# Block attention with a gated convolution MLP in fp32r on one Trainium2 core: units of 512 tokens without halo instead of 288 tokens with it

## The chip, the cores and the metric

One core of one Trainium2 chip runs the kernel. The metric is the device time of one execution in microseconds (us), from several executions of the compiled program; beside it one execution was recorded by the hardware profiler. Engines: TensorE (PE), VectorE (DVE), ScalarE (ACT), GpSimd (POOL), and SyncE (SP), whose queue issues all DMAs here. PSUM has eight banks of 512 fp32 columns; SBUF holds everything else.

## The reference

q, k and v are (8, 8, 576, 64): batch, heads, tokens, head width. Each chunk of 64 tokens attends to itself, and the heads side by side are the input (512 wide) of an MLP with a gate from a convolution over three tokens, which stops at the ends of each batch entry (576 tokens):

```python
scores = scale * np.matmul(q_c, k_c.transpose(0, 1, 2, 4, 3))     # 64 x 64 per chunk and head
attn = softmax(scores)                                            # max taken away, sum + 1e-9
x = (attn @ v_c), heads side by side                              # (8, 576, 512)
h = np.maximum(x @ w_in, 0.0)                                     # (8, 576, 1024)
conv_out[s] = sum over k of conv_w[k] * hp[s + k]                 # hp: h with a zero token at both ends
out = h * (1 / (1 + np.exp(-conv_out))) @ w_out                   # (8, 576, 512)
```

w_in, conv_w and w_out come as 64-bit floats and are split on the chip; the outputs are fp32.

## The kernel before, in words

The kernel works on 36 tiles of 128 tokens for the attention and the output, and on 16 units of 288 tokens (half a batch entry, `UNITS`, L49) for the first product and the gate. All 4608 tokens lie in one row.

Both products run in fp32r with each operand split into a high and a low half, three matmuls for one: high x high, high x low, low x high. The first product (`mm1`, L352) of a unit u and a block f of 128 of the 1024 hidden columns is 3 x 4 matmuls with wi as weights and x as moving tile; its 290 columns are the 288 tokens and 2 of the neighbour unit (`x_window`, L322), since the convolution needs the token beside. The result lies in one PSUM bank. From there: `h_relu` (ACT, in place), `c_mid` (ACT, middle tap), `c_left` and `c_right` (DVE, outer taps), `c_sig` (ACT, tanh of half), `c_mul` (DVE, (tanh + 1) * h, which frees the bank), `g_hi` (ACT, rounds to fp32r), `g_lo` (POOL, the rest, which frees the buffer c). g_h and g_l are rings of 640 tokens for each block (`GR`, L47). The second product (`mm2`, L410) of a tile t and a block f is three matmuls with 128 tokens of g as weights and 512 columns of wo as moving tile; eight steps f sum a tile up in one bank. `o_copy` (ACT) and `o_store` (SP) bring it out.

Attention of a tile: its q and k are turned (the first nine tiles on TensorE, `t_pe`, L170; later ones on DVE, `t_dve`), `scores` (L219: 32 matmuls of 64x64), softmax (`s_max`, `s_sub`, `s_sum`, `s_eps`, `s_rec` on DVE, `s_exp` on ACT, `s_norm`, `s_fold`, `s_scale` on POOL), the weights turned (on TensorE, `p_pe`; from tile 12 by DMA and DVE, `p_swap`, `p_dve`), `attn_v` (L302: 32 matmuls of 64x64), and `x_hi` (ACT) and `x_lo` (DVE) write the unit's moving tiles x_h and x_l, three units in turn (`NX`). A PSUM tile of two banks, `sx`, has two halves, each for the scores or the product of one tile. From tile 12 on a second one is lent from the banks (`give_up`, L212), and one step `both` (L316) multiplies the last pair with v and makes the scores of the next.

The weights (4 MB each of w_in and w_out as 64-bit words) are loaded and converted in the first 60 us: `w_load` (SP), `w_scale`, `w_hi` (ACT), `w_shift`, `w_words` (DVE), `w_left_g` (POOL).

What sets the order: `step` (L76) collects all steps with engine, buffers taken and freed, and the steps that they come after; `order_` (L751) is a list of their numbers written out by hand, which fixes the order of the instructions on each engine, SP's queue among them. The loop behind it (L875) hands out the buffers in that order (`room`, L516) and computes from planned costs where spare matmuls on the identity fill early idle time (L926, L929). Each engine takes its instructions strictly in this order.

Of the kernel before, what the change touches and what calls it, by code (L numbers as in the profile page):

```python
# [18 lines left out]
def attn_ffn(ctx: ExitStack, tc: tile.TileContext, q, k, v, w_in, conv_w, w_out, out):  # L31
# [10 lines left out]
    HS = S // 2  # L42
    CUTS0 = [0, HS]
    XU = HS + 2
    XS = XU + 2
    NX = 3
    GR = 5 * P  # L47
    NT = B * S // P
    UNITS = [(c0, c1) for b in range(B) for c0, c1 in zip(CUTS0 if b == 0 else [S * b, S * b + HS], (CUTS0 if b == 0 else [S * b, S * b + HS])[1:] + [S * b + S])]  # L49
    NU = len(UNITS)  # L50
    W_ROWS = set()
    NAT = 9
    TG = 3
    BOTH = 12
    PAIR = 12
    ONE_PAIR = True
# [6 lines left out]
    rawv = ctx.enter_context(tc.tile_pool(name="rawv", bufs=4))  # L63
    work = ctx.enter_context(tc.tile_pool(name="work", bufs=2))
    work3 = ctx.enter_context(tc.tile_pool(name="work3", bufs=3))
    work4 = ctx.enter_context(tc.tile_pool(name="work4", bufs=4))
    work1 = ctx.enter_context(tc.tile_pool(name="work1", bufs=1))
    work7 = ctx.enter_context(tc.tile_pool(name="work7", bufs=7))
# [18 lines left out]
    ps_y = ExitStack()  # L87
# [10 lines left out]
    x_h = const.tile([P, NX, KT, XS], F32R, name="x_h")  # L98
    x_l = const.tile([P, NX, KT, XS], F32R, name="x_l")
    g_h = const.tile([P, FT, GR], F32R, name="g_h")  # L100
    g_l = const.tile([P, FT, GR], F32R, name="g_l")
    cw = const.tile([P, 3 * FT], F32, name="cw")

# [97 lines left out]
    def sx_half(i):  # L201

        cols = slice(G * C * (i % 2), G * C * (i % 2) + G * C)
        return (sx if i // 2 else lent["pair"])[:, :, cols]
# [3 lines left out]

    def lend(st):
        pass  # L210

    def give_up(st):  # L212

        st["given"] = st.get("given", 0) + 1
        if st["given"] == 2:
            ps_y.close()
            st["pair"] = ctx.enter_context(tc.tile_pool(name="ps_z", bufs=1, space=PSUM)).tile([P, 2, 512], F32, name="z_ps")

    def scores(st):  # L219
# [18 lines left out]
    def s_sub(st):  # L238
        st["e"] = work3.tile([P, H, C], F32, name="e")
# [62 lines left out]
    def attn_v(st):  # L302
        for g in range(G):
            for s in range(2):
                for hp in range(2):
                    j0, n, m = C * (hp ^ s), hp, s
                    if st["t"] >= TP:
                        j0, n, m = C * s, hp, hp if st["t"] >= TP + 2 else hp ^ s
# [7 lines left out]
    def both(st, tiles, tiles_x):  # L316
        for a in tiles_x:
            attn_v(a)
# [3 lines left out]
    def x_window(u):  # L322

        a, z = UNITS[u]
        return a - (2 if a % S else 0), z + (2 if z % S else 0)

    def x_views(st, t, x):

        xv = sx_half(st.get("x", 2)).rearrange("p s (g i) -> p g s i", i=C)
        parts = []  # L330
        for s in range(2):
            t0 = C * (2 * t + s)
            for u in range(NU):
# [89 lines left out]

# [546 lines left out]
```

## Time and profile before

| | us |
|---|---|
| median of 3 executions | 492.94 |
| lowest and highest | 489.9, 494.02 |
| span of the profiled execution, first to last instruction | 488.9 |
| TensorE busy in it | 478.4 (98%) |
| VectorE, ScalarE, GpSimd busy | 342.6 (70%), 299.2 (61%), 192.0 (39%) |

The profiled execution has no time of its own beside its span; the median of the executions is 4.0 us longer than the span. Matmuls are pipelined and their ends are modelled, so lengths of neighbouring matmuls overlap; what one costs is the distance of the starts. An engine's busy time says little about an engine that is not the bound.

### The profile page before, as it was taken

The page shows a single profiled execution, that of the slowest core. Times are in us where ns is not written, and L with a number is a line of the kernel's source. Part 1 is how long each engine was busy: PE and PEld are TensorE (multiplying, and loading weights), DVE is VectorE, ACT ScalarE, POOL GpSimd, SP SyncE. Part 2 cuts the span into 40 slices and gives each one's busy share as a digit, 9 for nine tenths or more (in the row PEclk, how much of TensorE's full clock was granted, in tenths as well). Part 3 has the DMA queues.
Part 4 walks back from the last instruction along what each step waited for, and adds up shares of the span by engine and source line. Part 5 has one row for each costly group of instructions (what it writes and reads, how often), then busy time and mean ns, then how long its engine had stood idle before and what let it go on. Part 6 is the DMA issues. An engine that isn't in the chain of part 4 may idle for free.

```text
span 488.9 us, 12846 instructions
## 1 busy us (share of the span) xinstructions
PE 478.4 (98%) x4961; PEld 425.2 (87%) x4961; DVE 342.6 (70%) x726; ACT 299.2 (61%) x749; POOL 192.0 (39%) x261
## 2 busy tenths in 40 slices
PE   7799999999999999999999999999999999999996
PEld 4689899989899889898898999998889899998885
DVE  3789988767877788888778687978786655563300
ACT  4589997667564656765556566655654566565411
POOL 1245565252351635355242525352523155143120
PEclk9899999999999999999999999999999999999999
DMA  8998955234655744266565444547302002010012
GB/s 214 297 271 214 269 96 81 48 49 89 131 114 112 147 84 98 47 143 131 101 132 101 100 79 76 118 95 165 82 23 83 24 6 66 0 44 1 21 66 86
DMA packets 180610, 50.16 MB, mean 103 GB/s; under 512 B 164653, under 2 KB 172869, under 8 KB 180549
## 3 DMA queue, kind: packets, MB, share of 16 engines
q1 hardware_dynamic: 180548, 49.34, 44.2%
q8 instruction: 39, 0.64, 0.6%
q14 instruction: 23, 0.18, 0.1%
HBM read 36.72 MB, written 9.44 MB: 94 GB/s over the span
## 4 chain that ended last, share of the span: by engine, by line
PE 90%; DMA 4%; ACT 2%; DVE 2%; POOL 1%; issue 1%; SPq 0%; POOLq 0%; ACTq 0%
PE b_ps L414 42%; PE b_ps L360 39%; DMA qk<-in_k 3%; PE sx_ps L309 2%; PE sx_ps L226 2%; PE b_ps L177 2%; PE z_ps L309 1%; DMA w<-in_moe_w_out 1%; PE z_ps L226 1%; PE b_ps L295 1%; DVE wt L456 1%; POOL wi_l L460 1%; ACT wt L447 0%; ACT c L372 0%; SPq L121 0%
## 5 line engine op out<-in xcount | busy, mean ns | idle before, releaser
L405 POOL TENSOR_TENSOR g_l<-c,g_h 128x288 fp32r<-128x288 f32 (+8 forms) x184 | 110.1, 620 | 184.9 <-ACT g_h L401 155.6
L414 PE MATMUL b_ps<-wo_h,g_h 128*128 128x512 f32 x288 | 115.6, 402 | 0.0
L414 PE MATMUL b_ps<-wo_h,g_l 128*128 128x512 f32 x288 | 113.6, 394 | 0.0
L414 PE MATMUL b_ps<-wo_l,g_h 128*128 128x512 f32 x288 | 113.4, 394 | 0.0
L376 DVE SCALAR_TENSOR_TENSOR c<-b_ps,cw,c 128x287 f32<-128x287 f32 (+1 forms) x128 | 64.7, 509 | 55.1 <-ACT c L372 54.7
L360 PE MATMUL b_ps<-x_h,wi_h 128*128 128x290 f32 x512 | 90.3, 298 | 0.2 <-ACT qkT L195 0.2
L360 PE MATMUL b_ps<-x_l,wi_h 128*128 128x290 f32 x512 | 89.6, 297 | 0.0
L367 ACT ACTIVATE b_ps<-b_ps 128x290 f32<-128x290 f32 x128 | 50.8, 399 | 63.1 <-PE b_ps L360 62.8
L360 PE MATMUL b_ps<-x_h,wi_l 128*128 128x290 f32 x512 | 89.2, 296 | 0.0
L360 PEld LDWEIGHTS b_ps<-x_h,wi_h 128*128 128x128 f32 x512 | 80.2, 189 | 9.2 <-ACT qkT L195 0.4
L391 DVE SCALAR_TENSOR_TENSOR c<-c,b_ps 128x288 f32<-128x288 f32 x128 | 56.7, 446 | 35.7 <-ACT c L388 35.2
L388 ACT ACTIVATE c<-c 128x288 f32<-128x288 f32 x128 | 56.6, 444 | 41.0 <-DVE c L382 40.1
L360 PEld LDWEIGHTS b_ps<-x_l,wi_h 128*128 128x128 f32 x512 | 75.8, 190 | 0.0
L360 PEld LDWEIGHTS b_ps<-x_h,wi_l 128*128 128x128 f32 x512 | 75.4, 189 | 0.0
L372 ACT ACTIVATE c<-b_ps,cw 128x288 f32<-128x288 f32 x128 | 63.9, 501 | 9.7 <-POOL g_l L405 2.4
L382 DVE SCALAR_TENSOR_TENSOR c<-b_ps,cw,c 128x288 f32<-128x288 f32 (+1 forms) x128 | 64.8, 512 | 2.8
L414 PEld LDWEIGHTS b_ps<-wo_h,g_l 128*128 128x128 f32 x288 | 54.2, 188 | 12.7
L401 ACT CAST g_h<-c 128x288 fp32r<-128x288 f32 (+8 forms) x184 | 58.3, 355 | 7.1 <-PE b_ps L414 3.6
L414 PEld LDWEIGHTS b_ps<-wo_h,g_h 128*128 128x128 f32 x288 | 54.4, 189 | 8.6
L414 PEld LDWEIGHTS b_ps<-wo_l,g_h 128*128 128x128 f32 x288 | 54.2, 188 | 7.5
L271 POOL TENSOR_TENSOR wt<-wt,z 128x512 f32<-128x512 f32 x24 | 25.3, 1053 | 45.9 <-DVE z L262 18.6
L419 ACT ACTIVATE wt<-b_ps 128x512 f32<-128x512 f32 x36 | 21.4, 597 | 31.2 <-PE b_ps L414 31.1
(66 smaller groups left out, 467.8 us busy)
## 6 DMA issues: line engine op xcount, KB each, us to landing
out<-wt SPq DMA_DIRECT2D x36, 256.0 KB, 2.4
v<-in_v SPq DMA_DIRECT2D x21, 256.0 KB, 3.5
qk<-in_q SPq DMA_DIRECT2D x96, 48.0 KB, 2.3
qk<-in_k SPq DMA_DIRECT2D x96, 48.0 KB, 2.2
w<-in_moe_w_out SPq DMA_DIRECT2D x4, 1024.0 KB, 6.4
wt<-wt SPq DMA_DIRECT2D x48, 64.0 KB, 2.0
qk<-in_k SPq DMA_DIRECT2D x96, 24.0 KB, 1.9
qk<-in_q SPq DMA_DIRECT2D x96, 24.0 KB, 1.9
```

The lines of the kernel that those rows point to most:

```text
L271: nc.gpsimd.tensor_tensor(out=two(st, "to"), in0=two(st, "of"), in1=z, op=ALU.mult)
L360: nc.tensor.matmul(h_ps[:, 0:hi - lo], lhsT=wt[:, f // 2, kt, P * (f % 2):P * (f % 2) + P], rhs=xt[:, u % NX, kt, 0:hi - lo], start=n == 0 ...
L367: nc.scalar.activation(out=h, in_=h, func=AF.Relu)
L372: nc.scalar.mul(out=st["c"], in_=banks[st["h"]][:, i0:i0 + st["n"]], mul=cw[:, FT + f:FT + f + 1])
L376: nc.vector.scalar_tensor_tensor(out=c[:, a:n], in0=banks[st["h"]][:, i0 + a - 1:i0 + n - 1], scalar=cw[:, f:f + 1], in1=c[:, a:n], op0=AL ...
L382: nc.vector.scalar_tensor_tensor(out=c[:, 0:b], in0=banks[st["h"]][:, i0 + 1:i0 + 1 + b], scalar=cw[:, 2 * FT + f:2 * FT + f + 1], in1=c[: ...
L388: nc.scalar.activation(out=st["c"], in_=st["c"], func=AF.Tanh, scale=0.5)
L391: nc.vector.scalar_tensor_tensor(out=st["c"], in0=st["c"], scalar=1.0, in1=banks[st["h"]][:, st["i0"]:st["i0"] + st["n"]], op0=ALU.add, op ...
L401: nc.scalar.copy(out=g_h[:, f, gs], in_=st["c"][:, cs])
L405: nc.gpsimd.tensor_tensor(out=g_l[:, f, gs], in0=st["c"][:, cs], in1=g_h[:, f, gs].bitcast(F32), op=ALU.subtract)
L414: nc.tensor.matmul(banks[st["o"]], lhsT=gt[:, f, o:o + P], rhs=wt[:, f, :], start=f == 0 and n == 0, stop=f == FT - 1 and n == 2)
L419: nc.scalar.mul(out=st["os"], in_=banks[st["o"]], mul=0.5)
```

## The change

The first product's units become 9 units of 512 tokens, four attention tiles each, with no neighbour tokens. Its matmuls have 512 columns and fill a bank; in unit 0 a block is made in two halves of 256 columns, the first of which needs tiles 0 and 1 only. The passes over a block run on the whole bank. The outputs of the tokens at a unit's ends, and of those beside a batch boundary within a unit, are made by another way: `rim_ends` and `rim_mid` (ACT) copy two tokens at each such place of h into a small tile `rim`, and once per unit `rim_steps` does the convolution, the gate and the split for four tokens in eight blocks at once with small operations (POOL: `r_mid`, `r_side`, `r_add`, `r_lo`; ACT: `r_sig`, `r_hi`; DVE: `r_mul`). The output tiles begin one token before a unit's tiles; the first and the last tokens share one tile, which is stored in two transfers at the end.

x_h and x_l keep two units instead of three, each row of 512 columns, so that all large tiles begin at one place mod 256 bytes (a row of x_h was 292 columns, 1168 bytes). The second `sx` tile is gone: scores and product of a pair are steps of their own, and all six other banks serve the products throughout. Pairs begin at tile 4. Buffers: c 7 to 3, wt 4 to 3, v 4 to 3, e 3 to 2, and two for the output (`os`). `order_` is a new list: the rows of tile 0 are loaded ahead of w_in, and the second product of a unit, up to four tiles in turn, stands between the first-product blocks of the next.

```diff
-    HS = S // 2
-    NX = 3
-    GR = 5 * P
+    UT = 4
+    UN = UT * P
+    NU = NT // UT
...
-    x_h = const.tile([P, NX, KT, XS], F32R, name="x_h")
-    g_h = const.tile([P, FT, GR], F32R, name="g_h")
+    x_h = const.tile([P, 2, KT, UN], F32R, name="x_h")
+    g_h = const.tile([P, FT, UN + P], F32R, name="g_h")
+    rim = const.tile([P, FT, 8 * NU + 8], F32, name="rim")
...
-    def both(st, tiles, tiles_x):
-        for a in tiles_x:
-            attn_v(a)
+    def scores_of(tiles):
         for a in tiles:
             scores(a)
+    def attn_of(tiles):
+        for a in tiles:
+            attn_v(a)
...
-    def mm1(st, u, f):
+    def mm1(st, u, f, c0, c1):
         n = 0
         for wt, xt in ((wi_h, x_h), (wi_h, x_l), (wi_l, x_h)):
             for kt in range(KT):
                 nc.tensor.matmul(
-                    h_ps[:, 0:hi - lo], lhsT=wt[:, f // 2, kt, P * (f % 2):P * (f % 2) + P], rhs=xt[:, u % NX, kt, 0:hi - lo],
+                    banks[st["h"]][:, c0:c1], lhsT=wt[:, f // 2, kt, P * (f % 2):P * (f % 2) + P], rhs=xt[:, u % 2, kt, c0:c1],
                     start=n == 0, stop=n == 3 * KT - 1)
...
+    def rim_ends(st, u, f):
+        h, r = banks[st["h"]].rearrange("p (a b) -> p a b", b=2), rim[:, f, 8 * u:8 * u + 8].rearrange("p (a b) -> p a b", b=2)
...
+            nc.scalar.copy(out=r[:, 0:4:3, :], in_=h[:, 0:UN // 2:UN // 2 - 1, :])
+    def rim_mid(st, u, f):
+        m = (S - UN) * u
+        n = min(m + 2, UN) - (m - 2)
+        nc.scalar.copy(out=rim[:, f, 8 * u + 2:8 * u + 2 + n], in_=banks[st["h"]][:, m - 2:m - 2 + n])
...
+    def r_add(st, k, n):
+        i = slice(0, 2) if n == 0 else slice(k // 2, k // 2 + 1)
+        c = st["rc"][:, :, n, i]
+        nc.gpsimd.tensor_tensor(out=c, in0=c, in1=st["rt"][:, :, n, i], op=ALU.add)
...
     def o_store(st, t):
-        nc.sync.dma_start(out=out_rows[P * t:P * t + P, :], in_=st["os"])
+        if t is None:
+            nc.sync.dma_start(out=out_rows[0:P - 1, :], in_=st["os"][1:P, :])
+            nc.sync.dma_start(out=out_rows[P * NT - 1:P * NT, :], in_=st["os"][0:1, :])
+            return
+        nc.sync.dma_start(out=out_rows[t:t + P, :], in_=st["os"])
...
-    room = {"slot": 2, "wslot": 2, "sx": 4, "bk": 6, "grp": 2, "v": 4, "qkT": 2, "m": 2, "e": 3, "z": 2, "pT": 2, "c": 7, "wt": 4,
-            "wv": 2, "we": 1}
+    room = {"slot": 2, "wslot": 2, "sx": 2, "bk": 6, "grp": 2, "v": 3, "qkT": 2, "m": 2, "e": 2, "z": 2, "pT": 2, "c": 3, "wt": 3, "os": 2, "rc": 2}
...
+    def attend(tiles, writes):
+        sts = [st_ for st_, _, _, _ in tiles]
...
+        s = step("PE", 0.47 * len(tiles), key, scores_of, (sts,), [a for _, tt, _, _ in tiles for a in tt],
+                 take=[("sx", st_, "s") for st_ in sts], free=["qkT"] * len(tiles), bank="sx")
+        ends = soft_all(sts, s, key)
+        s = step("PE", 0.47 * len(tiles), key, attn_of, (sts,), [a for a in ends] + [v_ for _, _, v_, _ in tiles],
+                 take=[("sx", st_, "x") for st_ in sts], free=["pT", "v"] * len(tiles), bank="sx")
+        for st_ in sts:
+            t = st_["t"]
+            a = step("ACT", 0.58, key + 1, x_hi, (st_, t), [s] + writes, bank="sx")
+            x_done[t] = step("DVE", 0.69, key + 1, x_lo, (st_, t), [a], free=[("sx", "x")], bank="sx")
...
     def block(key, u, f, after):
+        if u == 0:
+            s = step("PE", 1.43, key, mm1, (st, u, f, 0, UN // 2), wi_done[f] + [x_done[0], x_done[1]], take=[("bk", st, "h")])
+            s = step("PE", 1.43, key, mm1, (st, u, f, UN // 2, UN), [s, x_done[2], x_done[3]])
+        else:
+            s = step("PE", 2.73, key, mm1, (st, u, f, 0, UN), wi_done[f] + [x_done[t] for t in range(UT * u, UT * u + UT)], take=[("bk", st, "h")])
...
+        s = g = step("ACT", 0.62 if u else 0.8, key + 2.5, g_hi, (st, u, f), [s] + [mm2_of[u - 1, j, f] for j in range(UT) if (u - 1, j, f) in mm2_of])
+        s = step("POOL", 1.37 if u else 1.55, key + 2.5, g_lo, (st, u, f), [s], free=["c"], port=True)
...
+    sets = [[t] for t in range(4)] + [[t, t + 1] for t in range(4, NT, 2)]
...
     order_ = [
-        0, 30, 12, 72, 91, 31, 32, 33, 13, 1, 14, 77, 15, 73, 16, 36, 74, 75, 2, 4, 17, 3, 92, 76, 110, 5, 6,
+        71, 0, 1, 72, 2, 90, 3, 4, 5, 6, 74, 7, 11, 73, 75, 12, 17, 8, 9, 91,
...
```

In the new list, decoded: TensorE's order in the head is the turning of tiles 0 to 5, the scores of tiles 0 to 3, the products of tiles 0 to 2, the first half block (f = 1), the product of tile 3, the next half block. SP's order is the rows of tile 0, conv_w, the rows of tile 1, the two halves of the first quarter of w_in, the rows of tile 2, v of 0, the rows of 3, half of the second quarter, v of 1, the other half, the rows of 4 and 5, v of 2, the third quarter, v of 3, the last quarter, the rows of 6, v of 4, half of w_out, v of 5, the rows of 7, the other half of w_out, v of 6, the rows of 8. Between a pair's product with v and the next pair's scores stand, from tile 12 on, four steps of the second product, or one block of the first product, or more of both. The last unit's first-product blocks end 18 steps of the second product before the first step that needs `rim_steps` of that unit.

## Rows read from the trace of the kernel before

**Rows 1.** The page of the profile, its head: the span, and each engine's busy time with its share of the span and its count of instructions.

```profile
span 488.9 us, 12846 instructions
...
PE 478.4 (98%) x4961; PEld 425.2 (87%) x4961; DVE 342.6 (70%) x726; ACT 299.2 (61%) x749; POOL 192.0 (39%) x261
```

**Rows 2.** The table by stage: the stretch in us and its length, busy time of PE, PEld (weight loads), DVE, ACT and POOL with their counts, the granted TensorE clock, the busy share of the DMA engines and the GB/s that they moved.

```profile
0.00:20.00 20.00, 14.30 (x173) 9.84 (x175) 10.62 (x22) 9.61 (x15) 4.04 (x10) 0.98 0.92 261
20.00:40.00 20.00, 19.23 (x334) 17.07 (x331) 15.73 (x31) 16.45 (x31) 9.77 (x7) 0.94 0.95 268
40.00:60.00 20.00, 19.75 (x308) 17.93 (x307) 19.10 (x41) 19.26 (x43) 11.15 (x9) 1.00 0.98 237
60.00:80.00 20.00, 20.00 (x187) 18.40 (x187) 17.01 (x36) 18.10 (x45) 11.82 (x11) 1.00 0.54 95
...
200.00:240.00 40.00, 40.00 (x466) 35.84 (x465) 32.72 (x69) 24.26 (x62) 19.00 (x29) 1.00 0.55 114
```

**Rows 3.** The chain that ended last, in order of time: start in us, length in us, what it is and of how many instructions.

```profile
135.74 4.84 PE b_ps L360 x36
...
225.35 5.58 PE b_ps L414 x24
...
461.30 23.81 PE b_ps L414 x102
```

**Rows 4.** The timeline of TensorE in the head: start in us, length in us, line, what it writes and reads, shape, count, and in brackets idle time before it with its releaser. L177 and L182 turn q and k, L360 is the first product.

```profile
8.67 2.98 PE L177 MATMUL b_ps<-ident,qk 128*64 128x128 f32 x48 [1.62 <-DMA qk<-in_k]
...
17.88 4.40 PE L177 MATMUL b_ps<-ident,qk 128*64 128x128 f32 x48 [2.37 <-DMA qk<-in_k]
...
31.60 0.78 PE L360 MATMUL b_ps<-x_h,wi_h 128*128 128x290 f32 x4
...
37.74 0.60 PE L182 MATMUL b_ps<-ident,qk 128*128 128x128 f32 x4
38.09 0.78 PE L360 MATMUL b_ps<-x_h,wi_h 128*128 128x290 f32 x4
```

**Rows 5.** The costliest groups of the page, the first third of each product: line, engine, operation, out<-in, shape, count, then busy us, mean ns of one, and idle time before. The two other thirds of each product have the same counts.

```profile
L414 PE MATMUL b_ps<-wo_h,g_h 128*128 128x512 f32 x288 | 115.6, 402 | 0.0
...
L360 PE MATMUL b_ps<-x_h,wi_h 128*128 128x290 f32 x512 | 90.3, 298 | 0.2 <-ACT qkT L195 0.2
```

**Rows 6.** The timeline of TensorE around one visit to the attention (L309 the product with v, L226 the scores, two tiles of each).

```profile
218.12 0.40 PE L414 MATMUL b_ps<-wo_h,g_l 128*128 128x512 f32 x1
218.45 0.69 PE L309 MATMUL z_ps<-pT,v 64*64 64x64 f32 x32
...
219.43 0.65 PE L226 MATMUL sx_ps<-qkT 64*64 64x64 f32 x32
219.90 0.65 PE L226 MATMUL z_ps<-qkT 64*64 64x64 f32 x32
220.47 0.50 PE L414 MATMUL b_ps<-wo_h,g_h 128*128 128x512 f32 x1
220.81 0.39 PE L414 MATMUL b_ps<-wo_l,g_h 128*128 128x512 f32 x1
```

**Rows 7.** The timeline of SP's queue in the head: each row is the issue of DMAs.

```profile
0.73 0.96 SPq L434 DMA_DIRECT2D w<-in_moe_w_in  x2
1.73 0.76 SPq L121 DMA_DIRECT2D qk<-in_q  x1
...
10.76 0.63 SPq L121 DMA_DIRECT2D qk<-in_q  x1
```

**Rows 8.** Groups of instructions of the other engines, shapes kept apart: columns as in rows 5. L372, L376 and L391 are passes over a block, L401 and L405 make g_h and g_l, L345 and L349 make x_h and x_l, L460 makes the low half of a weight.

```profile
L372 ACT ACTIVATE c<-b_ps,cw 128x288 f32<-128x288 f32 x128 | 63.9, 501 | 9.7 <-POOL g_l L405 2.4 <-ACT b_ps L367 0.4
...
L391 DVE SCALAR_TENSOR_TENSOR c<-c,b_ps 128x288 f32<-128x288 f32 x128 | 56.7, 446 | 35.7 <-ACT c L388 35.2
...
L376 DVE SCALAR_TENSOR_TENSOR c<-b_ps,cw,c 128x288 f32<-128x288 f32 x64 | 32.4, 508 | 31.7 <-ACT c L372 31.5
...
L349 DVE TENSOR_TENSOR x_l<-sx_ps,x_h 128x512 fp32r<-128x512 f32 x14 | 9.3, 673 | 3.8 <-ACT x_h L345 3.8
...
L345 ACT CAST x_h<-sx_ps 128x512 fp32r<-128x512 f32 x14 | 8.2, 592 | 2.9 <-PE sx_ps L226 2.6 <-PE sx_ps L309 0.2
...
L349 DVE TENSOR_TENSOR x_l<-sx_ps,x_h 128x256 fp32r<-128x256 f32 x13 | 5.2, 415 | 0.7 <-ACT x_h L345 0.7
L460 POOL TENSOR_TENSOR wi_l<-wt,wi_h 128x512 fp32r<-128x512 f32 x4 | 5.1, 1291 | 11.1 <-DVE wv L479 8.5 <-ACT qkT L193 1.9 <-DVE wt L456 0.7
...
L405 POOL TENSOR_TENSOR g_l<-c,g_h 128x32 fp32r<-128x32 f32 x16 | 4.1, 254 | 12.4 <-ACT g_h L401 12.4
...
L401 ACT CAST g_h<-c 128x32 fp32r<-128x32 f32 x16 | 3.4, 213 | 1.0 <-DVE c L391 0.7
```

**Rows 9.** The costliest groups of the page: all pieces of g_l and of g_h, of several lengths.

```profile
L405 POOL TENSOR_TENSOR g_l<-c,g_h 128x288 fp32r<-128x288 f32 (+8 forms) x184 | 110.1, 620 | 184.9 <-ACT g_h L401 155.6
...
L401 ACT CAST g_h<-c 128x288 fp32r<-128x288 f32 (+8 forms) x184 | 58.3, 355 | 7.1 <-PE b_ps L414 3.6
```

**Rows 10.** The timeline at the end, ScalarE: the last two output tiles are copied.

```profile
484.44 1.30 ACT L419 ACTIVATE wt<-b_ps 128x512 f32<-128x512 f32 x2 [0.75 <-PE b_ps L414]
```

**Rows 11.** The timeline of ScalarE behind the visit of rows 6: the casts to x_h of the two tiles that were multiplied there.

```profile
223.40 0.59 ACT L345 CAST x_h<-z_ps 128x512 fp32r<-128x512 f32 x1
...
226.08 0.59 ACT L345 CAST x_h<-sx_ps 128x512 fp32r<-128x512 f32 x1
```

More of the change, by code (lines that the diff above doesn't have):

```diff
@@ L578, in att @@
-        if old:
-            s = step("PE", 0.47 * len(new + old), key, both, (new[0][0], [n[0] for n in new], [o[0] for o in old]), after,
-                     take=take, free=free, bank="sx")
-        else:
-            s = step("PE", 0.47, key, scores, (st,), after, take=take, free=free, bank="sx")
-        before["s"] = s
-        for b, tb, _, writes_b in old:
-            x_steps(b, tb, s, key, writes_b)
-        if t == PAIR - 1:
-            a = step("POOL", 0.0, key, give_up, (lent,), [s], take=[("bk", lent, ("y", 0))])
-            step("POOL", 0.0, key, give_up, (lent,), [a], take=[("bk", lent, ("y", 1))], free=[("sx", "l0"), ("sx", "l1")])
@@ L589, in att @@
[L589 to L603 removed]
+        return st, tt, ldv
@@ L637, in x_steps @@
[L637 to L643 removed]
+            return [step("POOL", 1.05, key + 3, s_scale, (st,), [n], free=["z"], port=True)]
@@ new lines, in attn_ffn @@
+        for set_ in sets:
+            if u < NU and set_[0] // UT == u:
+                writes = [mm1_of[u - 2, f] for f in range(FT)] if u > 1 else []
+                tiles = [(*att(t, key_of[t], 0.1 + 0.5 * t if t < 5 else 4.5 + t), key_of[t]) for t in set_]
+                attend(tiles, writes)
+        for f in range(FT):
+            if u < NU:
+                g_of[u, f] = block(U[u] + (U[u + 1] - U[u]) * f / FT, u, f, [])
+        if u and u < NU:
+            rim_steps(U[u + 1] + 3, u)
@@ L735, in attn_ffn @@
+    st, prev = {}, None
+    for f in range(FT):
+        key = U[NU] + 40 + 0.7 * f
+        prev = step("PE", 0.68, key, mm2, (st, UN, f), [prev, g_of[0, f][1], rim_done[NU - 1, 1]] + wo_done[f], take=[("bk", st, "o")] if f == 0 else [])
+    s = step("ACT", 0.6, key + 1, o_copy, (st,), [prev], take=["os"], free=[("bk", "o")])
+    step("SP", 0.9, key + 2, o_store, (st, None), [s], free=["os"], lag=0.8)
     early = {"DVE": 0.083, "ACT": 0.092, "PE": 0.0, "POOL": -0.075, "SP": -0.05}
     late = {"DVE": 0.035, "ACT": 0.035, "PE": 0.035, "POOL": 0.1, "SP": 0.1}
-    kinds = {scores: 1, attn_v: 1, both: 1, p_pe: 2, t_pe: 2, c_pe: 2}
+    kinds = {scores_of: 1, attn_of: 1, p_pe: 2, t_pe: 2, c_pe: 2}
```

332 lines of the change are left out of this document (147 added, 185 removed), and 219 rows, old and new, of the table order_.

## The prediction

> **What bounds the kernel now.** I read the busy shares and slices first, then the table by stage, then the chain that ended last, then single stretches. The page says that TensorE is busy 98% of a span of 488.9 us, with the next engine, VectorE, at 70% [rows 1]. A busy matmul row is modelled and overlaps its neighbour, so busy alone proves little. What proves it is the stages: from 60 us to 470 us TensorE has no idle time in any window (20.00 of 20.00, 40.00 of 40.00), while in 200 to 240 us VectorE works 32.72 of 40, ScalarE 24.26 and GpSimd 19.00 [rows 2]. And in the chain in order of time the long pieces are runs of the two products: 36 matmuls of 290 columns in 4.84 us, 24 of 512 in 5.58 us, 102 of 512 in 23.81 us [rows 3]. So the kernel is a row of matmuls without gaps from 31.6 us, where the first product begins [rows 4], to 485 us, with a head before and a tail of some 4 us behind. The head is the only stretch with another limit: the DMA engines are busy 92% to 98% for the first 60 us at 237 to 268 GB/s [rows 2], and TensorE waits there for q and k (2.37 us before 17.88 us) [rows 4].
>
> From these pieces one matmul of the first product costs 4.84/36 = 134.3 ns and one of the second 5.58/24 = 232.5 ns from start to start. There are 3 x 512 and 3 x 288 of them [rows 5]: 206.3 us and 200.9 us.
>
> The time is the median 492.9 us, the span of the profiled execution 488.9 us; I take the 4.0 us between them as unchanged and work in differences.
>
> **First product, 290 to 512 columns.** Of 1536 matmuls, 960 remain: 8 units x 8 blocks x 12 = 768 of 512 columns, and 192 of 256 in unit 0, whose blocks are cut in two. No row shows this product at 512 columns. Granted clock 1.00 [rows 2] is the 2.4 GHz level, 0.417 ns a cycle; if a column takes one cycle, 290 columns take 120.8 ns and 13.5 ns come on top. Lower end: this surplus is per matmul, so 512 columns cost 213.3 + 13.5 = 226.8 ns. Upper end: it is per column, 134.3 x 512/290 = 237.1 ns. The second product's row, 232.5 ns, lies between, with a surplus of 19.2 ns. I take 226.8 ns: same weights, same moving tile, and 13.5 ns is already a mean over starts at every multiple of 16 bytes, since a row of x_h is 1168 bytes now. At 256 columns, 106.7 + 13.5 = 120.2 ns. 768 x 0.2268 + 192 x 0.1202 = 174.2 + 23.1 = 197.3 us, so -9.0 us (ends: 237.1 and 118.5 ns, -1.5; 224, -11).
>
> **Second product, tiles at one place mod 256 bytes.** Count and width stay. By the shapes, x_h and x_l are 14016 bytes, 192 over a multiple of 256, so g_h now stands 128 bytes off wo_h; afterwards all big tiles begin at one place. No row shows that this place costs anything: the surplus of 19.2 against 13.5 ns may be place or width. Ends: 226.8 ns (-4.9 us) if place is all of it, 232.5 (0) if none, 238 (+4.9) if the common place is the worse one. I take half, -2.5 us.
>
> The Trainium skill (TensorE: Matmul & The Clock Gate, section Back-to-back issue gap) gives N/2.4 + 2.5 ns for a warm matmul, 123 ns at 290 columns and 216 ns at 512. The trace disagrees: 134.3 and 232.5 ns. By that page's figures the two products would together take some 373 us after the change, an estimate; what would have to hold for it is the last rival below.
>
> **Attention steps.** Scores and the product with v now go in separate steps of one pair. Each visit to the 64x64 matmuls costs beyond its work: the matmul before it is followed after 0.33 instead of 0.23 us, the first one after it is followed after 0.34 instead of 0.23, and the last group is stretched (219.90 to 220.47 us, 0.57 where the group before it takes 0.47) [rows 6]: about 0.33 us. Before there are 12 + 11 + 13 = 36 visits, afterwards 20 + 20 = 40: +1.3 us.
>
> **Head.** The rows of tile 0 are now loaded ahead of w_in; before, 1 MB of w_in is issued first, at 0.73 us [rows 7], about 4 us of DMA at 261 GB/s [rows 2]. Tile 0 is turned from 8.67 us, and tile 2, whose load waits for its place until 10.76 us, only at 17.88 us [rows 4, 7]; both should come some 3 to 4 us earlier. The first half-width block needs only tiles 0 and 1 instead of 0 to 2. Against this, the new order of TensorE has the attention of tile 3 right after the first half block, and its v is the 7.0th MB in the queue: at 257 GB/s it lands near 29.5 us. By then TensorE has also done what now comes behind 31.6 us: tile 5 turned (two times four transposes, 0.35 us for four from start to start), four more transposes, and a half block of 1.4 us [rows 4]. So it stands 2.1 us earlier with 2.5 us more done, 4.6 us ahead, of which waits for the v of tile 5 (11.0 MB) and the rows of tiles 7 and 8 take back about 1.8. ScalarE and VectorE work 80% to 96% of 20 to 60 us [rows 2] and convert the weights in the same time, so I book -2 us (ends -5 and +2).
>
> **Work of the other engines** does not grow. At 512 columns an x_h cast takes 0.59 us, x_l 0.67 us, and 256 columns fewer save 0.26 us [rows 8]. From this slope three VectorE passes make 0.74 + 0.74 + 0.67 = 2.15 us for a block, x72 = 155 us, where 128 x (0.51 + 0.51 + 0.45) = 188 us is spent now; ScalarE four passes of about 0.63 plus two rim copies of 0.21, 2.9 us x72 = 211 us, where 128 blocks x four passes of 0.36 to 0.50 us stand now, 184 to 256 us; GpSimd 1.29 us (the row of w_left at 512) x72 = 93 against 110 us, plus 8 rounds of about nine small operations near 0.25 us, 18 us in all [rows 8, 9]. None is on the path: TensorE spends some 48 us on a unit (96 matmuls of each product, 44 us, and four tiles of attention). The rim round itself stands, on GpSimd, in front of the last two g_lo of its unit and in the last unit in front of two output tiles; there 18 steps of the second product (12 us) lie between the last first-product block and the first step that needs it, and its chain is about 10 us. Cost 0; without this cover 2 us once.
>
> **Waits that the change adds.** The pair's scores share two halves of one PSUM tile with the product before them, so scores wait until x_lo of the pair before is done. Queued behind on TensorE is everything. The order leaves 12 matmuls of 512 columns, 2.7 us, at seven places and 3.4 us or more at the rest; two x_h and two x_l take 2.5 us [rows 8]. I book 2 us for 16 pairs. Buffers c go from 7 to 3; a c is held about 5.4 us by the durations above, so three serve a block each 1.8 us, below the 2.7 us of a block. Behind a c_mid that waits for one stand ScalarE's casts and o_copy; the price is 0 while TensorE has second-product steps in between, and is bounded by the slower rival.
>
> **Tail.** Now ScalarE copies the last two tiles (484.44 us, 1.30 us) and SP stores [rows 10]; afterwards the last two tiles end together and the last store is two transfers: +0.5 us.
>
> Sum: -9.0 - 2.5 + 1.3 - 2 + 2 + 0.5 = -9.7 us, span 479.2, time 483.2 us.
>
> **Rivals.**
> *Nothing from width or place.* Both products at 232.5 ns, head unchanged: -4.6 + 0 + 1.3 + 0 + 2 + 0.5 = -0.8, time 492. For it: 232.5 is the only row of this width, in the tail too, where nothing else runs (23.81/102 = 233.4 ns). Against: the first product's surplus is smaller.
> *Larger gain.* A common place takes the second product to 226.8 as well, the head gives 5, scores never wait: -9.0 - 4.9 + 1.3 - 5 + 0.5 = -17.1, time 476. For it: the head is bound by what is loaded first.
> *Slower: scores wait for x_lo.* Place: between a pair's product with v and the next scores. In before the pair multiplied at 218.45 us is cast only at 223.40 and 226.08 us, because casts stand in ScalarE's order behind other work [rows 6, 11]; there nothing waits for it. If the second x_lo comes 4.5 us after the product, TensorE loses 1.75 us at seven places and about 1.1 at nine, 22 us in place of my 2: +10.3, time 503. It decides from 0.73 us a pair (11.7/16). Against: in 200 to 240 us VectorE has 18% and ScalarE 39% free [rows 2].
> *The surplus was all place.* With one place for all tiles a matmul would cost only its columns: 184.3 us for each product, -22.0 - 16.6 + 1.8 = -36.8, time 456. Against: a surplus stands in both rows, with fixed and with changing places. The formula of the Trainium skill's page on TensorE (section Back-to-back issue gap) would come nearest to this.
>
> **Chances.** Forecast (478 to 488) 0.55, of which 0.02 within 1%; nothing from width 0.13; larger gain 0.20; scores wait 0.09; all place 0.03. A measurement of this kernel tells about 1% from no change, 4.9 us. Faster 0.53 + 0.20 + 0.03 = 0.76, same 0.15, slower 0.09. The range 474 to 492 leaves out the last two rivals.
>
> **What would show it.** Runs of first-product matmuls in the chain at 2.72 us for 12 (2.79 if width gives nothing); runs of 24 second-product matmuls at 5.44 to 5.51 us instead of 5.58; the first product starting at 26 to 30 us; idle time of TensorE before the scores lines, released by x_lo, below 2 us in all. Idle TensorE of over 10 us behind 60 us, or matmuls of 512 columns at 237 ns, would prove the forecast wrong.

## The result and the profile after

The changed kernel is slower by 0.7%: 495.9 us against 492.7 us in the median of 13 runs each, ratio 1.0072 (95% interval 1.0055 to 1.009). One of the runs before took 937.9 us; it does not enter the ratio. The forecast was 483, the range 474 to 492, so the time lies outside and on the other side. In the profiled executions the span went from 488.9 [rows 1] to 494.9 us, 6.0 us where the medians differ by 3.2. In every run with both numbers the time is 1.8 us longer than the span (496.71 and 494.9 us for the one profiled here), so the 488.9 us belong to about 490.7 us, a run 2.0 us below its median: of the 4.0 us between median and span before, only 1.8 are fixed. Differences of single spans below are uncertain by some 2 us for this reason.

The page's head and the table by stage (columns as in rows 2):

```profile
span 494.9 us, 11257 instructions
...
PE 470.2 (95%) x4383; PEld 387.5 (78%) x4383; DVE 318.2 (64%) x554; ACT 273.6 (55%) x617; POOL 176.5 (36%) x229
```

```profile
0.00:20.00 20.00, 15.06 (x199) 11.67 (x203) 9.14 (x21) 8.57 (x15) 3.67 (x10) 0.99 0.75 219
20.00:40.00 20.00, 17.32 (x361) 15.03 (x357) 12.98 (x23) 13.71 (x23) 6.96 (x6) 0.93 0.94 240
...
200.00:240.00 40.00, 40.00 (x294) 32.77 (x293) 30.76 (x56) 24.49 (x59) 18.56 (x25) 1.00 0.41 85
...
481.00:483.00 2.00, 0.00 (x0) 0.00 (x0) 0.00 (x0) 0.00 (x0) 0.00 (x0) 1.00 0.40 138
483.00:490.00 7.00, 0.00 (x0) 0.00 (x0) 0.00 (x0) 0.00 (x0) 0.00 (x0) 0.55 0.06 23
490.00:493.00 3.00, 0.00 (x0) 0.00 (x0) 0.00 (x0) 0.00 (x0) 0.00 (x0) 0.50 0.07 26
```

TensorE is busy 8 us less than before, as it was meant to be, and still the span is longer. The last three rows say where: behind 481 us no engine computes, and from 483 to 493 us the DMA engines are busy 6 to 7% at 23 to 26 GB/s. One sixteenth is 6.25%, the share of one DMA engine of 16 at work. The timelines (SyncE in the head, TensorE at the first product and around one visit to the scores, ScalarE, TensorE and SyncE at the end) and the chain in order of time:

```profile
8.94 0.61 SPq L98 DMA_DIRECT2D qk<-in_q  x1
...
32.80 0.74 PE L308 MATMUL b_ps<-x_h,wi_h 128*128 128x256 f32 x4
...
222.89 0.39 PE L427 MATMUL b_ps<-wo_h,g_l 128*128 128x512 f32 x1
223.20 1.16 PE L191 MATMUL sx_ps<-qkT 64*64 64x64 f32 x64
224.30 0.50 PE L427 MATMUL b_ps<-wo_h,g_h 128*128 128x512 f32 x1
224.63 0.39 PE L427 MATMUL b_ps<-wo_l,g_h 128*128 128x512 f32 x1
...
479.67 1.28 ACT L432 ACTIVATE os<-b_ps 128x512 f32<-128x512 f32 x2 [4.84 <-PE b_ps L427]
479.87 0.39 PE L427 MATMUL b_ps<-wo_h,g_l 128*128 128x512 f32 x1
...
480.97 0.26 SPq L436 DMA_DIRECT2D out<-os  x1
481.29 4.13 SPq L437 DMA_DIRECT2D out<-os  x1
```

```profile
353.96 8.16 PE b_ps L308 x36
...
426.54 8.16 PE b_ps L427 x36
```

TensorE's last matmul in the kernel before:

```profile
484.70 0.40 PE L414 MATMUL b_ps<-wo_h,g_l 128*128 128x512 f32 x1
```

Both products now run at 8.16/36 = 226.7 ns a matmul, where the second took 232.5 before [rows 3]. TensorE's last matmul ends at 480.3 us, 4.8 earlier than before (485.1). From there to the end of the span it is 14.6 us instead of 3.8. The store issued at 480.97 us is the last output tile that is stored: 127 rows from partition 1 on; the one issued at 481.29 is its partition 0, the last token.

### The profile page after: what moved, and what is told of

It is laid out like the page before. It is cut to its first block, busy times and chain, and to the rows that moved or that the text cites. A ratio compares the mean times of both kernels' runs of the same rounds, so it can differ in the third digit from the quotient of the medians.

```text
span 494.9 us, 11257 instructions
## 1 busy us (share of the span) xinstructions
PE 470.2 (95%) x4383; PEld 387.5 (78%) x4383; DVE 318.2 (64%) x554; ACT 273.6 (55%) x617; POOL 176.5 (36%) x229
## 4 chain that ended last, share of the span: by engine, by line
PE 81%; DVE 7%; DMA 4%; ACT 3%; issue 2%; SPq 0%; POOL 0%; ACTq 0%
PE b_ps L427 38%; PE b_ps L308 34%; PE sx_ps L274 3%; PE sx_ps L191 3%; DMA qk<-in_k 2%; PE b_ps L154 1%; DMA v<-in_v 1%; DVE c L345 1%; DMA w<-in_moe_w_in 1%; DVE c L361 1%; DVE c L351 1%; DVE m L201 1%; ACT g_h L372 1%; DVE wt L469 1%; DVE wt L464 0%
## 5 line engine op out<-in xcount | busy, mean ns | idle before, releaser
L376 POOL TENSOR_TENSOR g_l<-c,g_h 128x510 fp32r<-128x510 f32 (+1 forms) x80 | 79.2, 998 | 178.3 <-ACT g_h L372 115.7
L308 PE MATMUL b_ps<-x_h,wi_h 128*128 128x512 f32 (+1 forms) x320 | 80.7, 374 | 0.9 <-ACT qkT L172 0.6
L308 PE MATMUL b_ps<-x_l,wi_h 128*128 128x512 f32 (+1 forms) x320 | 78.8, 368 | 0.0
L308 PE MATMUL b_ps<-x_h,wi_l 128*128 128x512 f32 (+1 forms) x320 | 78.7, 368 | 0.0
L345 DVE SCALAR_TENSOR_TENSOR c<-b_ps,cw,c 128x510 f32<-128x510 f32 x72 | 53.1, 740 | 36.2 <-ACT c L340 28.7
L361 DVE SCALAR_TENSOR_TENSOR c<-c,b_ps 128x510 f32<-128x510 f32 (+1 forms) x72 | 48.1, 672 | 29.2 <-ACT c L357 21.7
L308 PEld LDWEIGHTS b_ps<-x_h,wi_h 128*128 128x128 f32 x320 | 56.1, 188 | 11.8 <-ACT qkT L172 0.9
L427 PEld LDWEIGHTS b_ps<-wo_h,g_h 128*128 128x128 f32 x288 | 54.1, 188 | 11.9
L427 PEld LDWEIGHTS b_ps<-wo_h,g_l 128*128 128x128 f32 x288 | 54.1, 188 | 11.5
L357 ACT ACTIVATE c<-c 128x510 f32<-128x510 f32 (+1 forms) x72 | 45.5, 635 | 20.7 <-DVE c L351 20.4
L351 DVE SCALAR_TENSOR_TENSOR c<-b_ps,cw,c 128x510 f32<-128x510 f32 (+1 forms) x72 | 53.0, 740 | 2.1 <-ACT rim L325 0.7
L372 ACT CAST g_h<-c 128x510 fp32r<-128x510 f32 (+1 forms) x80 | 44.9, 578 | 16.9 <-DVE c L361 13.0
L340 ACT ACTIVATE c<-b_ps,cw 128x510 f32<-128x510 f32 (+1 forms) x72 | 49.6, 692 | 1.8 <-ACT b_ps L315 0.4
L432 ACT ACTIVATE os<-b_ps 128x512 f32<-128x512 f32 x36 | 21.4, 601 | 31.3 <-PE b_ps L427 27.7
```

Of the source, the lines that this page charges most:

```text
L308: nc.tensor.matmul(banks[st["h"]][:, c0:c1], lhsT=wt[:, f // 2, kt, P * (f % 2):P * (f % 2) + P], rhs=xt[:, u % 2, kt, c0:c1], start=n == ...
L340: nc.scalar.mul(out=st["c"], in_=banks[st["h"]][:, i0:i0 + n], mul=cw[:, FT + f:FT + f + 1])
L345: nc.vector.scalar_tensor_tensor(out=c[:, a:n], in0=banks[st["h"]][:, i0 + a - 1:i0 + n - 1], scalar=cw[:, f:f + 1], in1=c[:, a:n], op0=AL ...
L351: nc.vector.scalar_tensor_tensor(out=st["c"], in0=banks[st["h"]][:, i0 + 1:i0 + 1 + n], scalar=cw[:, 2 * FT + f:2 * FT + f + 1], in1=st["c ...
L357: nc.scalar.activation(out=st["c"], in_=st["c"], func=AF.Tanh, scale=0.5)
L361: nc.vector.scalar_tensor_tensor(out=st["c"], in0=st["c"], scalar=1.0, in1=banks[st["h"]][:, i0:i0 + n], op0=ALU.add, op1=ALU.mult)
```

## The experiments

Where two kernels are compared, "cut store" is the changed kernel with its last store cut into 112 + 15 + 1 rows and nothing else.

**1. The store of 127 rows, cut.** My theory after the trace was that 127 rows are moved by one engine; the rival, that two late stores or the store of one row cost the time.

```diff
-            nc.sync.dma_start(out=out_rows[0:P - 1, :], in_=st["os"][1:P, :])
+            for a, n in ((1, 112), (113, 15)):
+                nc.sync.dma_start(out=out_rows[a - 1:a - 1 + n, :], in_=st["os"][a:a + n, :])
             nc.sync.dma_start(out=out_rows[P * NT - 1:P * NT, :], in_=st["os"][0:1, :])
```

> The changed kernel, with its last store of 127 rows cut into one of 112 and one of 15 rows, beside the one of 1 row; all else as it is. Theory A (a store of 127 rows is moved by one DMA engine alone, and the 10.8 us that the changed kernel ends later behind its last matmul are this): the stretch from the last matmul to the end falls from 14.6 us to about 4 us, the span from 494.9 to about 484.5, the time to about 485.5, 1.5% below the kernel before. Rival B (what costs is that two stores follow one another at the end, or that the store of one row is slow): three stores instead of two, so no gain, 495 to 497 us.

Measured: 486.5 us, ratio 0.9874 (0.9853 to 0.9896), span 482.9. SyncE's timeline and the table by stage at the end:

```profile
479.42 0.84 SPq L437 DMA_DIRECT2D out<-os  x2
480.32 0.24 SPq L438 DMA_DIRECT2D out<-os  x1
```

```profile
480.00:481.00 1.00, 0.00 (x0) 0.00 (x0) 0.00 (x0) 0.00 (x0) 0.00 (x0) 1.00 0.96 315
481.00:482.00 1.00, 0.00 (x0) 0.00 (x0) 0.00 (x0) 0.00 (x0) 0.00 (x0) 0.79 0.14 47
```

These rows, with those of the 128-row store issued just ahead, go at 315 GB/s with 96% of the engines busy. From the last matmul (478.7) to the end it is 4.2 us. Three stores instead of two cost nothing, so the rival falls.

**2. Without the store of one row.** The second line of the diff above is left out, the 127 rows stay.

> The changed kernel without its last store of 1 row (the row of token 4607 is left out of the output); the store of 127 rows stays. Theory A (the 127 rows go through one DMA engine): nothing gained, span 494 to 495 us. Rival B (the store of one row, or the second store behind the first, is what is late): about 10 us less, span near 485.

Measured: 495.8 us in one run, span 494.0. The 127 rows alone make the tail:

```profile
483.00:490.00 7.00, 0.00 (x0) 0.00 (x0) 0.00 (x0) 0.00 (x0) 0.00 (x0) 0.50 0.07 25
```

**3. 126 rows and 1 row.** As in 1, with ((1, 126), (127, 1)).

> The changed kernel with its last store of 127 rows cut into 126 rows and 1 row: almost the same transfer, one row shorter. Theory A in its sharp form (the number of DMA engines is the largest one up to 16 that divides the number of rows: 14 for 126, 1 for 127): the 126 rows take 9 packets of 84 ns on each of 14 engines, the tail falls to about 4 us as in the cut 112 + 15, span about 484.5, time about 485.5. Rival C (long stores to these rows of the output are slow, or one engine serves whatever follows the last matmul): unchanged, 495 to 497 us.

Measured: 486.0 us, ratio 0.9896 (0.986 to 0.9932), span 483.2. One row less in the transfer, and the table shows again 96% of the DMA engines at 313 GB/s:

```profile
480.00:481.00 1.00, 0.00 (x0) 0.00 (x0) 0.00 (x0) 0.00 (x0) 0.00 (x0) 1.00 0.96 313
```

So neither the size nor the place in the output matters, but the number 127. The Trainium skill has this rule (DMA: Bandwidth & Descriptors, section Why a DMA increments its semaphore by 16 and not by 1): a transfer is spread over the largest number of engines up to 16 that divides its rows, and 127 partitions get one. The trace agrees: 127 packets of 2 KB at 84 ns each are 10.7 us, and the tail grew by 10.8. The counts of packets behind 470 us agree too. The kernel before (four stores of 128 rows), experiment 2 (three of 128 and one of 127) and experiment 3 (three of 128, then 126, 1 and 1) have:

```profile
DMA packets 578, 1.07 MB, mean 41 GB/s; under 512 B 64, under 2 KB 64, under 8 KB 576
DMA packets 560, 1.05 MB, mean 40 GB/s; under 512 B 49, under 2 KB 49, under 8 KB 560
DMA packets 576, 1.05 MB, mean 40 GB/s; under 512 B 64, under 2 KB 64, under 8 KB 576
```

Beside the 2 KB of each row there are small packets (under 512 B): 64/4 = 16 for a store of 128 rows, so 49 - 48 = 1 for 127 rows and 64 - 48 - 1 - 1 = 14 for 126. These are the numbers of engines that the rule gives.

**4. The same cost put into the kernel before.** Its store of the last tile is done as 127 rows and 1 row.

```diff
+        if t == NT - 1:
+            nc.sync.dma_start(out=out_rows[P * t:P * t + P - 1, :], in_=st["os"][0:P - 1])
+            nc.sync.dma_start(out=out_rows[P * t + P - 1:P * t + P, :], in_=st["os"][P - 1:P])
+            return
```

> The kernel before with one edit: its last store of 128 rows is done as 127 rows and 1 row, as the changed kernel has it. Theory A (127 rows go through one DMA engine): 127 packets of 84 ns one behind the other, 10.7 us, in place of 8 packets on each of 16 engines, 0.7 us; about +10 us behind the last matmul, span about 499, ratio about 1.021. Rival (something else in the changed kernel's last stage, such as its two tiles ending together, makes the late store slow): +0 to +1 us, ratio 1.000 to 1.002.

Measured: ratio 1.0166 (1.0126 to 1.0206), span 498.9. From the last matmul (487.1) to the end 11.8 us instead of 3.8. That is 8 and not 10 us, because this tile is not the last that is stored in the kernel before: its store is issued 3.5 us ahead of the end of the matmuls. SyncE's timeline, and the DMA issues of the last 17 us (KB each, median us to landing):

```profile
483.58 0.26 SPq L423 DMA_DIRECT2D out<-wt  x1
483.88 3.69 SPq L424 DMA_DIRECT2D out<-wt  x1
487.68 2.12 SPq L426 DMA_DIRECT2D out<-wt  x3
```

```profile
out<-wt SPq DMA_DIRECT2D x3, 256.0 KB, 9.1
```

The 127 rows are issued at 483.58 us, and the three ordinary stores behind them land only 9.1 us after their issue instead of 2.0 to 2.3, which fits that each has rows on the engine that is occupied. The tail is settled by 1 to 4.

**5. Place alone, in the kernel before.** An unused tile of 128 bytes moves g_h and g_l to the place of w_out mod 256.

```diff
+    const.tile([P, 32], F32, name="pad")
     g_h = const.tile([P, FT, GR], F32R, name="g_h")
```

> The kernel before with one edit: an unused tile of 128 bytes in each partition ahead of g_h, so that the g tiles of the second product lie at the same place mod 256 bytes as the weights w_out (before: 128 bytes off). Width, units and order stay. Theory P (of the second product's gain, place is the whole): the mean start to start of its matmuls falls from 232 to about 228 ns, 864 x 4.2 = 3.6 us less, ratio about 0.993. Rival W (the gain came with the new order and units, place does nothing): 232 ns as before, ratio 1.000 +- 0.002.

Measured: 489.2 us, ratio 0.9938 (0.9921 to 0.9955). The chain in order of time shows the second product (L415 here) at 23.16/102 = 227.1 ns against 233.4 [rows 3], the first (L361) unchanged at 134.2:

```profile
403.02 4.83 PE b_ps L361 x36
...
459.46 23.16 PE b_ps L415 x102
```

Over all its matmuls that stand between two others the mean start to start fell from 232.2 to 229.4 ns (the median from 232 to 227), which is 864 x 2.8 = 2.4 us, as much as the span fell (488.9 to 486.5); by the ratio the time fell by 2.2 to 3.9 us. Place is real, with new units or without; W falls.

**6. Place undone, in the changed kernel.** With the cut store, the tiles are created in another order, so that all x and g tiles lie 128 bytes off the weights mod 256 (shortened):

```diff
+    wi_h, wi_l, wo_h, wo_l = ...
     ident = const.tile([P, P], F32, name="ident")
...
-    wi_h, wi_l, wo_h, wo_l = ...
+    cw = const.tile([P, 3 * FT], F32, name="cw")
     x_h = const.tile([P, 2, KT, UN], F32R, name="x_h")
```

> The changed kernel with the last store cut into 112 + 15 + 1 rows, and the order of the tiles in memory changed so that the x and g tiles lie 128 bytes off the weights mod 256 (in the changed kernel: at the same place). Nothing else. Theory P (place is worth about 5 ns per matmul whose weights and moving tile are 128 bytes apart, in the second product as in the first): the start to start of the second product rises from 228 to about 232 ns (+3.6 us), that of the first from 227 to about 232 (+3.6 us) and the 256-column ones from 119.6 to about 124 (+0.8 us), together about +8 us on TensorE, time 486.5 -> 494, ratio near 1.003. Rival Q (only the second product, where x is not concerned): +3.6 us, ratio near 0.995. Rival W (place does nothing here): ratio 0.987 as without it.

Measured: 493.2 us, ratio 1.0012 (0.9995 to 1.003), against 0.985 to 0.987 for the cut store. The chain:

```profile
358.22 8.37 PE b_ps L308 x36
...
459.57 27.90 PE b_ps L427 x120
```

Both products now take 232.5 ns a matmul (8.37/36, 27.90/120). The matmuls of 256 columns do not rise: their mean is 118.6 ns against 119.5. So P holds at 512 columns in both products, and not at 256. Only these two distances, 0 and 128 bytes, were run. That the effect goes by the distance mod 256 bytes, and not by another number or by the place of one tile alone, is not shown.

**7. Fewer visits to the turns.** With the cut store, four of TensorE's turns of the normalised scores are moved behind their pair's other one, for tiles 4 to 11. In TensorE's order, decoded, for the first pair:

```diff
-mm1(0,3) p_pe(5) mm1(0,2) p_pe(4)
+mm1(0,3) mm1(0,2) p_pe(5) p_pe(4)
```

> The changed kernel with the last store cut into 112 + 15 + 1 rows, and four of the turns of the normalised scores on TensorE moved to stand directly behind their pair's other one (tiles 4 and 5, 6 and 7, 8 and 9, 10 and 11), so that TensorE leaves the products four times less; same instructions. Theory V (each visit of the attention between products costs about 0.37 us beside its matmuls): 43 visits become 39, about 1.5 us less on TensorE, time about 485.0, ratio 0.984 against 0.987 without it. Rival S (the turn that now comes later delays the attention's chain, and the next scores or products wait for it): as much or more is lost as idle time, ratio 0.987 or above.

Measured: ratio 0.9891 (0.9869 to 0.9913), no gain. TensorE's timeline of one merged visit:

```profile
67.79 0.66 PE L260 MATMUL b_ps<-ident,e 128*128 128x128 f32 x4 [0.33 <-DVE c L361]
69.21 0.63 PE L260 MATMUL b_ps<-ident,e 128*128 128x128 f32 x4 [0.77 <-ACT pT L265]
```

The two turns now wait 0.33 and 0.77 us. The second is released by the copy of the first out of its bank (L265, on ScalarE), so what the merged visit waits for is a free bank. This is idle time as large as S says, by another wait than S names. And V was wrong for this kind of visit: beside the two products around it, a visit of four turns takes 0.45 us and one of eight 0.87 in the kernel before, so there was nothing to save.

**8. v ahead of the rows that wait.** With the cut store, SyncE's order is changed at two places (decoded):

```diff
-load_rows(2) load_v(0) load_rows(3) w_load load_v(1)
+load_v(0) load_rows(2) load_v(1) load_rows(3) w_load
```

> The changed kernel with the last store cut into 112 + 15 + 1 rows, and in SyncE's order the loads of v for tile 0 ahead of the rows of tile 2 and for tile 1 ahead of the rows of tile 3, where SyncE stands waiting for a slot. Theory H (the head loses its time where SyncE's queue stands at the rows of tile 2 until 8.9 us with nothing left to transfer): the DMA share of the first 20 us rises from 0.75 to about 0.85, the rows of tile 4 are issued about 2 us earlier (from 17.8 to about 16), the first matmul of the first product comes 1 to 2 us earlier than 32.8, time 485 us, ratio about 0.984. Rival N (the head is bound by the bytes and by the attention chain of the first tiles): first product within 0.5 us of before, ratio 0.987.

Measured: ratio 0.9887 (0.9864 to 0.991), no gain, and the first product starts at 34.1 us. The table by stage and SyncE's timeline:

```profile
0.00:20.00 20.00, 15.88 (x242) 12.32 (x244) 9.34 (x22) 9.34 (x16) 3.70 (x10) 1.00 0.75 222
```

```profile
8.86 0.62 SPq L98 DMA_DIRECT2D qk<-in_q  x1
...
17.84 1.29 SPq L98 DMA_DIRECT2D qk<-in_q  x2
```

The DMA share of the first 20 us stays 0.75, and the rows of tile 4 are issued at 17.8 us as in the changed kernel (17.8). H falls. What holds these rows is not the place of tile 2: SyncE stands 2.4 us at the load of w_in ahead of them, until VectorE gives back a place for weights (L470), and issues them right behind it; in the changed kernel its issues follow one another almost without a pause from 8.94 us to them. Both edits in one kernel:

> Both of the last two edits and the cut store in one kernel, as the version that might be best. Theories V and H both: about 3 us below the kernel with the cut store alone, time about 483.5, ratio 0.981. If only one of them holds: 0.984. If neither: 0.987.

Measured: ratio 0.9909 (0.9889 to 0.9929). Neither holds.

**9. Twelve more visits.** With the cut store, from tile 12 on the products with v of a pair are two steps with one step of the MLP's products between them (decoded):

```diff
-attn_of(12, 13) mm1(2,3)
+attn_of(12) mm1(2,3) attn_of(13)
```

> The changed kernel with the last store cut into 112 + 15 + 1 rows, and from tile 12 on the attention's products with v of each pair in two visits of 32 matmuls with one product between them, instead of one visit of 64: the same instructions, 12 more visits. Theory V2 (a visit of the 64x64 matmuls costs about 0.36 us beside its matmuls: two visits of 64 take 2 x 1292 ns in the changed kernel, one of 128 took 2224 ns in the kernel before; a visit of four 128x128 turns has no such price, 2 x 445 against 872 ns for eight, which is why four fewer of them gave nothing): 12 x 0.36 = +4.3 us, ratio 0.996 against 0.987 to 0.989 without it. Rival M (the cost goes by the matmuls, and the larger sum of the visits in the changed kernel has another cause): +0.0 to +0.5 us, ratio as without it.

Measured: ratio 1.0148 (1.0122 to 1.0173), over three times the loss that V2 said. The timeline of one pair, the waits (us in total, times, longest), and the chain and the table by stage around one late pair:

```profile
217.27 0.39 PE L427 MATMUL b_ps<-wo_h,g_l 128*128 128x512 f32 x1
217.59 0.69 PE L274 MATMUL sx_ps<-pT,v 64*64 64x64 f32 x32
218.22 0.50 PE L427 MATMUL b_ps<-wo_h,g_h 128*128 128x512 f32 x1
218.55 0.39 PE L427 MATMUL b_ps<-wo_l,g_h 128*128 128x512 f32 x1
```

```profile
PE sx_ps L191 <- DVE x_l L300: 5.9, 6, 2.5
```

```profile
152.32 1.30 DVE x_l L300 x2
...
153.66 1.16 PE sx_ps L191 x64
154.82 4.53 PE b_ps L427 x12
159.35 2.73 PE b_ps L308 x12
```

```profile
153.00:157.00 4.00, 3.34 (x70) 2.80 (x71) 4.00 (x8) 3.29 (x8) 2.17 (x2) 0.75 0.82 150
```

From the product before to the second one behind, a visit of 32 takes 1.28 us (217.27 to 218.55), less two products of 0.228 us 0.82; a visit of 64 takes 1.29 (222.89 to 224.63 in the changed kernel). Two of 32 are 0.36 us dearer than one of 64, so V2's price holds, 12 x 0.36 = 4.3 us. Of the span's 14.3 us more than with the cut store alone (482.7), 5.9 are scores that wait for x_lo, the mechanism of my slower rival: the second half comes later, so its x_lo does. And behind the longest of these waits the granted clock of 153 to 157 us is 0.75: TensorE has stood for 2.5 us, and its next 12 matmuls of 512 columns take 4.53 us, 377 ns each, part of them at the lower of the two levels (1.2 and 2.4 GHz), before it is 2.73 us for 12 again. By the matmuls that take about 427 ns this costs some 3 us at two places. The three together are about 13 of the 14.3 us.

**10. The width undone.** With the cut store, each first product of 512 columns is done as two of 256.

```diff
+        if c1 - c0 == UN:
+            mm1(st, u, f, 0, UN // 2)
+            mm1(st, u, f, UN // 2, UN)
+            return
```

> The changed kernel with the last store cut into 112 + 15 + 1 rows, and each first product of 512 columns done as two of 256 columns (as unit 0 has them): 768 matmuls become 1536. Theory D (the gain of the first product is the width: 227.2 ns at 512 columns against 2 x 119.6 at 256): + 768 x 12.0 ns = +9.2 us, ratio 1.006. Rival (the weight loads and the matmuls' overhead are hidden and the gain of the first product had come from the columns of the halo alone, 580 becoming 576 for two units): +0, ratio 0.988.

Measured: ratio 1.0087 (1.007 to 1.0105), span 495.4, 12.7 above the cut store's. The chain, with the first product at 14.39/120 = 119.9 ns:

```profile
449.64 14.39 PE b_ps L312 x120
```

768 x (2 x 119.7 - 227.2) = 9.4 us is the width, as D says; of the rest, 1.9 us is a later start of the first product (33.2 against 31.3), 1.4 one wait before scores. The head's start scatters: 31.1 to 33.2 us in the kernels with the changed head and without the edit of 8.

**11. The cut store once more.**

> The changed kernel with the last store cut into 112 + 15 + 1 rows once more, beside the two others on the same chip, for a narrower interval on the version that beats both kernels: ratio 0.987 to 0.989 to the kernel before if the first result holds (486 to 487 us). If the first was luck of the head: 0.990 or more.

Measured: 484.7 us, ratio 0.9846 (0.9828 to 0.9864), span 482.7. This is below the 0.987 to 0.989 that were expected; the same kernel had 0.9874 in experiment 1. This version is faster than both kernels, 1.3 to 1.5% below the one before and, by the medians 484.7 and 495.9 of different sessions, 2.3% below the changed one.

## Why the prediction was wrong

**The tail, the step that failed.** "The last two tiles end together and the last store is two transfers: +0.5 us." It measured +10.8 us (14.6 against 3.8). I counted transfers and not rows: the diff says that the store has 127 rows, no row that I had read shows such a transfer, and I gave that operation one value instead of two bounds. With one engine's rate as the upper end, 127 rows at 84 ns, the term would have been +0.5 to +11, and slower than before a case with a chance. Experiments 1 to 4 show it from both sides; nothing else was needed to turn the sign, since with this store cut the kernel takes 484.7 to 486.5 us, 1.5 to 3.3 us above the 483.2 that I had forecast.

**First product: -9.0 forecast, -8.3 measured.** 1536 matmuls of 134.0 ns were 205.8 us; 768 of 227.2 and 192 of 119.7 are 197.5. The size came out, and the reason only for tiles at one place. There the surplus over 0.417 ns a column is about the same at 256, 290 and 512 columns (13.0, 13.2, 13.9 ns), as I took it. But experiment 6 shows that 512 columns cost 232.6 ns when x lies 128 bytes off, so 768 x 5.4 = 4.1 us of the 8.3 hang on the place, which I had given this term no part in; the rest is width. At 290 columns I see no such cost: sorted by the place of x mod 256, the matmuls of the kernel before have means of 131 to 136 ns, 133 at the weights' place and 131 at 128 bytes off. That the place came out well here was luck as far as this term goes.

**Second product: -2.5 forecast, -3.6 measured** (864 matmuls, 232.2 to 228.0 ns). I took half; place is the whole or nearly so: experiment 6 puts the matmuls back to 232.5 ns, experiment 5 takes 2.8 of the 4.2 ns away in the mean. With its neighbour in the sum: -11.9 against -11.5.

**Visits: +1.3 forecast, about +4.1 measured.** The price was right, 0.33 against 0.36 us (experiment 9), the count was not: I counted steps, 36 and 40, and took each for a visit. The 36 have the joint step of [rows 6] as one already; but behind the first product the 29 steps that are left of them stand in 23 stretches, since scores and products of single tiles also follow one another there, while the 33 that are left of the 40 stand in 33. So 10 visits came in, not 4. One joint visit shows the price: from 218.12 to 220.81 us [rows 6], 2.69, less two products 2.23 us, where the two visits after the change take 2 x 1.29. Behind 75 us there are 21 stretches without products before and 32 after, turns included, 34.4 and 38.5 us in all beyond the products. The price belongs to the 64x64 matmuls; visits of 128x128 turns have none that I can see (experiment 7). The Trainium skill (TensorEngine Tiling (Array Packing), section Key Properties) says that a change of tiling mode drains TensorE. The trace agrees as far as the price goes: 0.36 us for a visit to 64x64 tiles, none for one to the whole array; that it is a drain no run here shows.

**Head: -2 forecast; it gave none.** The first product starts at 32.8 us, not at 26 to 30. The rows of tile 2 are issued at 8.94 us instead of 10.76 [rows 7], but the DMA share of the first 20 us is 0.75 instead of 0.92 [rows 2]. Experiment 8 excludes SyncE's order around v as the cause. In it SyncE stands 2.4 us at a load of w_in until VectorE gives back a place for weights; whether this, or SyncE's 0.6 us for each issue, sets the pace of the head is not shown.

**Scores that wait for x_lo: +2 forecast, under 0.2 measured** (TensorE's list of waits has no such row). The slower rival was wrong for this kernel, and its mechanism exists: experiment 9 calls it up. Other waits of TensorE behind the first product took its place, 0.4 to 0.7 us each at 34, 47, 53 and 64 us.

In sum TensorE ends 4.8 us earlier: -11.9 for the products, +4.1 for the visits behind 75 us, +1.8 for those ahead of 75 us (12.4 to 14.2 us beyond the products, with these waits), +1.2 for the start (31.6 to 32.8 us, within its scatter). The forecast for the same point was -10.2. The profiled run before was 2.0 us below its median, as said above, and the one after 0.8 above, so between typical runs TensorE ends some 7 to 8 us earlier, an estimate from the medians (3.2 us slower in spite of 10.8 us more behind the last matmul).

## What to carry to other kernels

Before a store changes its number of rows, look at the factors of the new number: 127 rows cost 10 us more than 126 and 1 where nothing follows to hide them. Count switches to 64x64 matmuls in TensorE's order as stretches, not as steps, and price the stretch by the rows around it. Where two widths are compared, fix the places of weights and moving tiles first: here 128 bytes mod 256 were worth as much (4.1 us) as going from 290 to 512 columns (4.2 us).

## What the runs showed of the hardware

- A store of 127 rows runs at 23 to 26 GB/s, one of 126 or 112 rows beside others at 313 to 315 in the microsecond shown. Behind it SyncE's next issue takes 3.69 to 4.13 us (0.24 behind other stores), and ordinary stores queued behind it land after 9.1 us.
- A store of 127 rows has one small packet, one of 126 has 14, one of 128 has 16.
- A matmul of 512 columns takes 227 ns where the moving tile lies at the weights' place mod 256 bytes and 232.5 at 128 bytes off, in both products; at 256 columns place adds nothing (119.5 and 118.6 ns).
- A visit to 64x64 matmuls between products costs 0.36 us beside its work; a visit of 128x128 turns has no such price (0.45 us for four, 0.87 for eight).
- Behind a stand of TensorE of 2.5 us (to 153.66 us) the granted clock of 153 to 157 us was 0.75, and the next 12 matmuls of 512 columns took 4.53 instead of 2.73 us.
